# Re-placed weight loads, a 0/1 table for the head gates, and a swapped layout for half of K and V in a gated attention and FFN kernel

## The chip, the cores and the metric

The kernel runs on one core of one Trainium2 chip. The metric is device time in microseconds (us) of that core for one execution. Three runs of the kernel before the change gave 264.25, 263.18 and 264.29, so the median is 264.25. The profile comes from one more execution, which took 264.48; its span (first to last recorded instruction) is 262.7.

## The reference

With x of shape (1, 2048, 512) in bf16, the output is g * a + (1 - g) * b, where g = sigmoid(sum(x * gate_w)) per token.

- b is a gated FFN: `relu(x @ W_gate) * (x @ W_up) @ W_down`, with 1792 hidden columns.
- a is attention with a compressive memory over 4 segments of 512 tokens, 32 heads of width 16:

```python
for s in range(N):
    logits = q_s k_s^T * scale + mask            # causal within the segment
    a_dot = softmax(logits) @ v_s
    a_mem = (phi(q_s) @ M) / (phi(q_s) @ z + 1e-6)
    o_s = g_h * a_mem + (1 - g_h) * a_dot        # g_h = sigmoid(beta), one per head
    M = M + phi(k_s)^T v_s
    z = z + sum(phi(k_s))
a = concat(o_s) @ wo
```

Here phi(t) is t + 1 for t > 0, else exp(t).

## The kernel before the change

**Tiling.** The 2048 tokens are 4 segments (`seg`) of 512. A segment's 512 attention columns are 4 groups (`c`) of 128 columns, that is 8 heads of 16. A *unit* u = 4 * seg + c is one group in one segment, 16 in all. TensorE projects q and k transposed (columns on partitions), and v with tokens on partitions. One unit's heads lie in four 32-row blocks j of the 128 partitions, each with an even head (r = 0) and an odd one (r = 1).

**Scores.** `proj_k` (L567) casts the projected k into `ktr` and writes masked copies into `KT` (L578): the even heads' copy has the odd heads' rows at zero and the other way round, so that a 32-row matmul over a block gives one head's scores. A block of 128 keys has two halves of 64. `KT` holds five half blocks per key block: even half 0, even half 1, even half 0 again (the third masked copy, 256 columns), odd half 0, odd half 1. `qk` (L621) fills 2048 score columns in 4 PSUM banks, one *fill* for a parity r and a half k of the key blocks, four per unit. `qk_diag` (L632) computes for two units the first 64 queries of each key block against `KT[..., 2:4]`, half 0 of the even and of the odd head. `score` (L644) adds a fill or a diagonal to the plan together with the ACT exp that empties the banks (L648); since all of them use the same 4 banks, a score slot on TensorE waits for the exp of the slot before it. There are 72 score slots. GpSimd masks the fills (`mk`, L674): for the queries 64 to 127 of a key block it zeroes the keys that come later.

**PV.** `pv` (L689) multiplies the exps with V: for the fills with `Vp` (128 keys on the partitions, a column of ones behind the 16 of each head), for the diagonals with `Vm`, which `fill_vm` (L609) fills on VectorE from partitions 0 to 63 of `Vp`: even heads to partitions 0 to 63, odd heads to 64 to 127. PV's result is transposed and normalised on VectorE (L722 ff.). `memory` (L810) updates M and z from `pK` (phi(k), transposed by a DMA on SP, L591); `dens` and `recall` (L747, L777) compute the memory's part, with coefficients that go through DRAM on SP's queue (L773, L787).

**Gates.** exp(-beta) is computed on ACT (L401) for all 32 heads; `head_gates` (L385) makes 1/(1+e) and e/(1+e), `row_gates` (L390) picks for each 32-partition block the right heads by 20 small copies in all into `gcat`, and `pair_gates` (L397) spreads them into `bdg`.

**FFN.** `ffn_tasks` (L854): per segment 14 column blocks of gate and up projections (relu on ACT, product on VectorE, `hT`), then 4 token blocks of `out_tile` (L880), which adds hT @ wd and oT @ wo in one bank, scales it on VectorE and stores it.

**Loads.** They are issued ahead of the plan. SP's queue has x (columns 0 to 255 of segment 0, tokens 0 to 255), wq rows 0 to 127, the transposed x columns 256 to 511 (`dma_start_transpose`, L304), wk, wv, pieces of W_gate and W_up, gate_w, beta, the rest of x, the transposed x of segment 1, then `wd_sb` in two loads (L322) and `wo_sb` in seven (L323 to L327). ACT's queue has x (tokens 256 to 511), wq rows 128 to 255, and wq rows 256 to 511 in one load of 256 KB (`load_rows`, L306). The first two 128-column blocks of segment 0's x are turned on TensorE (`x0_tasks`, L498). `proj_q` (L542) for segment 0 runs as a first batch of 8 matmuls on these (wq blocks 0 and 1), and a second batch of 8 that needs the transposed load and wq blocks 2 and 3 (`got_q[2]`, L553).

**Order.** Every piece of work is a task (`plan.add`) with an engine, dependencies and an emit function. The tasks are numbered in the order in which they are added, and `ORDER` (L30) lists these numbers in the order in which they are emitted; each engine, and each DMA queue, runs its own tasks in that order. `UNITS` (L95) says which PSUM bank or ring buffer a task takes. Tasks with `flex` (projections and FFN) are emitted as one 128-column matmul (`full`, L469), or, when the TensorE task before left the array in column mode, as four matmuls of 32 columns side by side (L473). Scores run in row mode, PV, `memory` and `dens` in column mode, `recall` in a mode of its own. The task at L329 only stands for the time that the front loads take; it emits nothing.

Of the kernel before, what the change touches and what calls it, by code (L numbers as in the profile page):

```python
# [7 lines left out]
BF16 = mybir.dt.bfloat16  # L8
# [4 lines left out]
P = 128  # L13
# [165 lines left out]
def kernel(  # L179
# [106 lines left out]
    def load_wd(a, b, name):  # L286
        return load(nc.sync, wd_sb[:, a:b, :],
                    B_W_down.rearrange("(c p) n -> p c n", p=P)[:, a:b, :], name)
# [691 lines left out]
```

## Time and profile before

| | |
|---|---|
| median of three runs | 264.25 us |
| the profiled execution | 264.48 us |
| its span | 262.7 us |
| TensorE matmuls: busy, instructions | 257.8 us (98%), 3828 |
| VectorE: busy, instructions | 204.9 us (78%), 472 |
| ScalarE: busy, instructions | 183.7 us (70%), 168 |
| GpSimd: busy, instructions | 64.2 us (24%), 168 |
| exp of scores, L648 | 64 x 1877 ns and 8 x 1876 ns |
| third masked K, L578 (128x256) | 16 x 298 ns |
| the other two masked K, L578 (128x512) | 16 x 368 ns and 16 x 348 ns |
| small copies of the gates, L393 and L395 | 4 x 161 ns and 16 x 182 ns |
| masks of the fills on GpSimd, L677 | 128 x 452 ns |
| issue of wd and wo on SP | from 21.41 us to 29.64 us |
| TensorE's first matmul on wd | 64.27 us |

How to read it: PE is TensorE, DVE VectorE, ACT ScalarE, POOL GpSimd, SP the engine that issues most DMAs (SPq is its queue). A busy TensorE is not one at its peak, because matmuls overlap and the ends of their rows are modelled: the distance between the starts of two matmuls tells more than the duration of one. A line such as L469 is that of the helper that issues the matmul; which tile it reads tells what it is for. A row in the waits names the waiting engine and line, what it waited for, the total, the number of times and the longest, in us.

### The profile page before, as it was taken

The page shows a single profiled execution, that of the slowest core. Times are in us where ns is not written, and L with a number is a line of the kernel's source. Part 1 is how long each engine was busy: PE and PEld are TensorE (multiplying, and loading weights), DVE is VectorE, ACT ScalarE, POOL GpSimd, SP SyncE. Part 2 cuts the span into 40 slices and gives each one's busy share as a digit, 9 for nine tenths or more (in the row PEclk, how much of TensorE's full clock was granted, in tenths as well). Part 3 has the DMA queues.
Part 4 walks back from the last instruction along what each step waited for, and adds up shares of the span by engine and source line. Part 5 has one row for each costly group of instructions (what it writes and reads, how often), then busy time and mean ns, then how long its engine had stood idle before and what let it go on. Part 6 is the DMA issues. An engine that isn't in the chain of part 4 may idle for free.

```text
span 262.7 us, 8841 instructions
## 1 busy us (share of the span) xinstructions
PE 257.8 (98%) x3828; PEld 117.4 (45%) x3828; DVE 204.9 (78%) x472; ACT 183.7 (70%) x168; POOL 64.2 (24%) x168
## 2 busy tenths in 40 slices
PE   8899999999999999999999999999999999999995
PEld 3344434454444454444444445444444444444454
DVE  2798999999995756959989789676998858688722
ACT  3199889999788678888486776878568759873000
POOL 8022732212321423232031223133121243121000
PEclk9999999999999999999999999999999999999999
DMA  6999984110711201200220111320110200311011
GB/s 146 337 304 323 273 192 53 22 24 10 116 25 52 92 22 39 76 2 2 80 41 4 56 20 36 110 85 2 24 57 3 56 2 22 102 30 73 2 42 42
DMA packets 31566, 19.72 MB, mean 75 GB/s; under 512 B 16040, under 2 KB 29992, under 8 KB 31528
## 3 DMA queue, kind: packets, MB, share of 16 engines
q1 hardware_dynamic: 30840, 18.64, 26.2%
q8 instruction: 30, 0.49, 0.9%
q10 hardware_dynamic: 688, 0.52, 0.9%
q14 instruction: 8, 0.07, 0.1%
HBM read 13.21 MB, written 2.55 MB: 60 GB/s over the span
## 4 chain that ended last, share of the span: by engine, by line
PE 94%; DMA 2%; DVE 2%; SPq 0%; issue 0%
PE ps L469 56%; PE ps L473 20%; PE ps L626 8%; PE ps L699 7%; DMA xT<-in_A_x_dram 2%; PE ps L639 1%; DVE QT L559 1%; PE ps L819 1%; PE ps L795 0%; PE ps L755 0%; SPq L266 0%; DVE KT L578 0%; DVE ktr L575 0%; DVE osr L895 0%
## 5 line engine op out<-in xcount | busy, mean ns | idle before, releaser
L648 ACT ACTIVATE E<-ps 128x2048 bf16<-128x2048 f32 x64 | 120.2, 1877 | 27.3 <-PE ps L626 18.8
L677 POOL TENSOR_SCALAR_AFFINE_SELECT E<-E 128x256 bf16<-128x256 bf16 x128 | 54.8, 452 | 169.8 <-ACT E L648 169.8
L869 DVE TENSOR_TENSOR hT<-ps,rgr 128x512 bf16<-128x512 f32 x56 | 38.0, 684 | 17.0 <-PE ps L469 12.6
L469 PE MATMUL ps<-xT,wu_sb 128*128 128x512 bf16 x168 | 45.9, 380 | 0.0
L469 PE MATMUL ps<-xT,wg_sb 128*128 128x512 bf16 x154 | 42.0, 380 | 0.0
L863 ACT ACTIVATE rgr<-ps 128x512 bf16<-128x512 f32 x56 | 32.5, 599 | 13.4 <-PE ps L473 6.9
L469 PE MATMUL ps<-wd_sb,hT 128*128 128x512 bf16 (+1 forms) x174 | 40.3, 354 | 0.0
L730 DVE STREAM_TRANSPOSE T<-ps 128x512 f32<-128x512 f32 x32 | 22.2, 707 | 7.8 <-PE ps L699 7.7
L626 PE MATMUL ps<-QT,KT 32*128 32x320 bf16 (+3 forms) x512 | 25.4, 273 | 0.1
L469 PEld LDWEIGHTS <-wu_sb 128*128 128x128 bf16 x168 | 15.1, 98 | 18.7 <-issue 2.7
L469 PEld LDWEIGHTS <-hT 128*128 128x128 bf16 x174 | 15.2, 98 | 17.1 <-issue 2.1
L469 PEld LDWEIGHTS <-wg_sb 128*128 128x128 bf16 x154 | 14.4, 98 | 17.7 <-issue 1.3
L895 DVE TENSOR_SCALAR osr<-ps,ngcol 128x512 bf16<-128x512 f32 (+2 forms) x18 | 12.2, 685 | 11.2 <-PE ps L473 5.7
L699 PE MATMUL ps<-E,Vp 128*17 128x320 bf16 (+3 forms) x512 | 19.3, 274 | 0.0
L626 PEld LDWEIGHTS <-KT 32*128 32x128 bf16 x512 | 7.6, 92 | 25.5 <-issue 24.2
L473 PE MATMUL ps<-xT,wg_sb 128*32 128x512 bf16 x280 | 18.6, 379 | 0.0
L648 ACT ACTIVATE Em<-ps 128x2048 bf16<-128x2048 f32 x8 | 15.0, 1876 | 5.0 <-PE ps L639 5.0
L473 PE MATMUL ps<-wd_sb,hT 128*32 128x512 bf16 (+1 forms) x312 | 17.8, 360 | 0.0
L469 PE MATMUL ps<-xT,wq_sb 128*128 128x512 bf16 x60 | 16.4, 382 | 1.0 <-DMA xT<-in_A_x_dram 1.0
L469 PE MATMUL ps<-wv_sb,xT 128*128 128x512 bf16 x62 | 16.9, 380 | 0.0
L559 DVE CAST QT<-ps 128x512 bf16<-128x512 f32 x16 | 10.7, 687 | 6.4 <-PE ps L469 6.2
L473 PE MATMUL ps<-xT,wu_sb 128*32 128x512 bf16 x224 | 15.1, 379 | 0.0
(102 smaller groups left out, 301.3 us busy)
## 6 DMA issues: line engine op xcount, KB each, us to landing
out_dram<-osr SPq DMA_DIRECT2D x15, 128.0 KB
wd_sb<-in_B_W_down_dram SPq DMA_DIRECT2D x2, 896.0 KB
xn<-in_A_x_dram SPq DMA_DIRECT2D x3, 512.0 KB
cdr<-coefs SPq DMA_DIRECT2D x6, 256.0 KB
xn<-coefs SPq DMA_DIRECT2D x6, 256.0 KB
wg_sb<-in_B_W_gate_dram SPq DMA_DIRECT2D x2, 512.0 KB
wu_sb<-in_B_W_up_dram SPq DMA_DIRECT2D x2, 512.0 KB
wg_sb<-in_B_W_gate_dram SPq DMA_DIRECT2D x2, 384.0 KB
```

The source lines that it names most:

```text
L469: nc.tensor.matmul(out, lhsT=lhsT, rhs=rhs, start=start, stop=stop)
L473: nc.tensor.matmul(out[r], lhsT=lhsT[:, r], rhs=rhs, start=start, stop=stop, tile_position=(0, 32 * j))
L559: prj["q", seg, c] = plan.add("DVE", 600, key - RQK, lambda: nc.vector.tensor_copy(QT[i][:], bank(sl)), [a], DVL, frees=[sl])
L626: nc.tensor.matmul(ps[:, j * L + o:j * L + o + L - q], lhsT=KT[i][rows, kb, 3 * r:3 * r + 2].rearrange("p h q -> p (h q)"), rhs=QT[i][rows ...
L639: nc.tensor.matmul(ps[:, o:o + HP], lhsT=KT[i][rows, kb, 2:4].rearrange("p h q -> p (h q)"), rhs=QT[i][rows, kb * P:kb * P + HP], start=Tr ...
L648: last_exp[0] = [plan.add("ACT", 66 + 4 * L / 1.2, key, lambda: nc.scalar.activation(dst, ps[:, 0:4 * L], ACT.Exp, scale=SCALE), [a] + war ...
L677: nc.gpsimd.affine_select(out=m[:, :, o:o + HP], in_=m[:, :, o:o + HP], compare_op=ALU.is_ge, fill=0.0, base=HP, pattern=[[0, 4], [1, HP]] ...
L699: nc.tensor.matmul(bank(sl)[32 * m:32 * m + HW, q:q + w], lhsT=(Vp[i] if n < 4 else Vm)[:, kb, r, 4 * c + j, 0:HW], rhs=rhs, start=(n == 0 ...
L730: done.append(plan.add("DVE", 633, key - RL, lambda r=r, sl=sl: nc.vector.transpose(T[ts.i][:, r], bank(sl)), [a] + done, 75 if r else 0, ...
L863: r = plan.add("ACT", 478, key - RL, lambda sl=gsl, rs=rs: nc.scalar.activation(rgr[rs.i][:], bank(sl), ACT.Relu), [g], ACL, frees=[gsl])
L869: nc.vector.tensor_tensor(hT[hs1.i][:], bank(sl), rgr[rs.i][:], ALU.mult)),
L895: nc.vector.tensor_scalar(osr[os.i][:, n0 - c0:n1 - c0], bank(sl)[:, 0:n1 - n0], ngcol[:, tt:tt + 1], None, ALU.mult)),
```

## The change

Four things are changed, and the order and the bank choice are written anew for them.

1. *Loads.* wq rows 256 to 511 are no longer one load on ACT's queue but two loads of 128 rows on SP's queue, behind the transposed x load. The second batch of the first q projection is split in two by wq block, so that each part waits for its own load. The loads of wd (two) and wo (four tasks) become tasks of the plan, on SP, placed by ORDER.
2. *Gates.* A 0/1 table `pick`, filled by GpSimd with 21 memsets, is multiplied with beta and reduced over the four blocks, so that each partition gets its own heads' beta; exp, 1/(1+e) and e/(1+e) are then computed on the picked values.
3. *K and V.* The even heads' K is stored with its two 64-key halves swapped. The two halves that the diagonal needs are then neighbours (`KT[..., 1:3]`), and the third masked copy goes. The even heads' V for the fills comes from a new tile `Vs` with the same swap, filled by two SBUF-to-SBUF DMAs per segment on SP, each of 64 partitions; the even heads' masks cover partitions 0 to 63 alone.
4. *Planner's figures.* Landing times (`LANDS`) and the placeholder for SP's front time are other numbers.

```diff
-    KT = [sb([P, 4, 5, P // 2], BF16, f"KT{i}") for i in range(RQ)]
+    KT = [sb([P, 4, 4, P // 2], BF16, f"KT{i}") for i in range(RQ)]
+    Vs = sb([P, 4, H // 2, 18], BF16, "Vs")
...
-    got_q = [load(eng, wq_sb[:, ci, :], A_wq[ci * P:(ci + 1) * P, :], "q%d" % ci)
-             for ci, eng in enumerate((nc.sync, nc.scalar))]
+    got_q = [load_wq(nc.sync, 0), load_wq(nc.scalar, 1)]
     nc.sync.dma_start_transpose(out=xT[0][:, NC // 2:NC, :], in_=x[0:L, halves[1]])
     got_x0b = arrival("x0")
-    got_q.append(load_rows(nc.scalar, wq_sb, A_wq, 1, "q"))
+    got_q += [load_wq(nc.sync, ci) for ci in range(2, NC)]
...
-    got_d = [load_wd(0, 7, "d0"), load_wd(7, NF, "d1")]
...
+    def load_late():
+        for j, (f0, f1) in enumerate(((0, 7), (7, NF))):
+            got_d.append(plan.add("SP", 1270, K(2 + j), lambda f0=f0, f1=f1: nc.sync.dma_start(
+                out=wd_sb[:, f0:f1, :],
+                in_=B_W_down.rearrange("(c p) n -> p c n", p=P)[:, f0:f1, :]),
+                lat=5000, xfer=2800.0))
...
+    nc.gpsimd.memset(pick[:], 0.0)
+    for m in range(4):
+        rows = slice(32 * m, 32 * m + 32)
+        nc.gpsimd.memset(pick[rows, 1, :, m], 1.0)
+        for c in range(NC):
+            nc.gpsimd.memset(pick[rows, 0, c, (m + c) % 4], 1.0)
...
+    def pick_heads():
+        nc.vector.tensor_tensor(
+            gsel.rearrange("p k c j r -> p k (c j r)"), pick.rearrange("p k c j r -> p k (c j r)"),
+            betab[:, None, :].to_broadcast([P, 2, H]), ALU.mult)
+        nc.vector.tensor_reduce(out=gcat.rearrange("p k c r -> p (k c) r"),
+                                in_=gsel.rearrange("p k c j r -> p (k c) r j"),
+                                axis=mybir.AxisListType.X, op=ALU.add)
...
     def head_gates():
+        nc.vector.tensor_scalar(rcat[:], gcat[:], 1.0, None, ALU.add)
+        nc.vector.reciprocal(rcat[:], rcat[:])
+        nc.vector.tensor_tensor(gcat[:, 0], gcat[:, 0], rcat[:, 0], ALU.mult)
...
-            a = matmuls(K(-4, c), [got_q[2]] + got_x[0][1], sl, proj_mm(wq_sb, c, 0)[2:], prev=a,
-                        start=False)
+            for ci in range(2, NC):
+                a = matmuls(K(-6 + ci, c), [got_q[ci]] + got_x[0][1], sl,
+                            [proj_mm(wq_sb, c, 0)[ci]], prev=a, start=False, stop=ci == NC - 1)
...
-            for n, (o, w, m, dur) in enumerate([(0, 2, mcol_e, 262), (3, 2, mcol_o, 262),
-                                                (2, 1, mcol_e, 165)])]
+            plan.add("DVE", 262, key + n, lambda n=n, m=m: nc.vector.tensor_scalar(
+                KT[u % RQ][:, :, 2 * n:2 * n + 2],
+                ktr[ks.i].rearrange("p (k h q) -> p k h q", k=4, h=2)[:, :, ::1 if n else -1],
+                m[:, 0:1],
...
+        att["vs", seg] = [plan.add("SP", 600, K(4 * seg - 2 - (1 if seg else 0), 2000), lambda h=h: (
+            nc.sync.dma_start(out=Vs[64 - 64 * h:128 - 64 * h], in_=Vp[i][64 * h:64 * h + 64, :, 0])),
+            [prj["v", seg, t] for t in range(4)] + [att.get(("pv", 4 * seg - 4 + c)) for c in range(NC)],
+            2500, xfer=400.0) for h in range(2)]
...
-        masks += [att["diag", u]] + att["vm", seg]
+        masks += [att["diag", u]] + att["vm", seg] + att["vs", seg]
...
-                            lhsT=(Vp[i] if n < 4 else Vm)[:, kb, r, 4 * c + j, 0:HW],
+                            lhsT=(Vm[:, kb, r] if n > 3 else Vp[i][:, kb, 1] if r else
+                                  Vs[:, kb])[:, 4 * c + j, 0:HW],
```

In the new ORDER, SP's tasks after the front loads begin with: pK of unit 0 (segment 0), the xn load of segment 1, the two V copies of segment 0, pK of unit 2, the second half of wd, three of the wo tasks, pK of unit 1, the transposed x of segment 2, then the first half of wd and the last wo task. The first score slot stands behind six matmuls of the v projection, where it stood right behind those of k.

More of the change, by code (lines that the diff above doesn't have):

```diff
@@ L321, with wo @@
     load_gu(3)
-    got_d = [load_wd(0, 7, "d0"), load_wd(7, NF, "d1")]
-    for c in range(NC):
-        n = P - 32 * c
-        nc.sync.dma_start(out=wo_sb[0:n, c, :], in_=A_wo[(c + 1) * P - n:(c + 1) * P, :])
-        if c:
-            nc.sync.dma_start(out=wo_sb[n:P, c, :], in_=A_wo[c * P:(c + 1) * P - n, :])
-    got_o = arrival("o")
-    plan.add("SP", 28300, -1e9, None, xfer=5900.0)
+    got_d, got_o = [], []
+    plan.add("SP", 22000, -1e9, None, xfer=4500.0)
+    def load_late():
[5 more added lines that the diff above has]
+        for c in range(NC):
+            def wo(c=c, n=P - 32 * c):
+                nc.sync.dma_start(out=wo_sb[0:n, c, :], in_=A_wo[(c + 1) * P - n:(c + 1) * P, :])
+                if c:
+                    nc.sync.dma_start(out=wo_sb[n:P, c, :], in_=A_wo[c * P:(c + 1) * P - n, :])
+            got_o.append(plan.add("SP", 1250 if c else 600, K(4, c), wo, lat=3500, xfer=450.0))
     ident = sb([P, P], BF16, "ident")
@@ L379 @@
     nc.gpsimd.memset(rcol[:], 0.0)
+    nc.gpsimd.memset(pick[:], 0.0)
+    for m in range(4):
+        rows = slice(32 * m, 32 * m + 32)
+        nc.gpsimd.memset(pick[rows, 1, :, m], 1.0)
+        for c in range(NC):
+            nc.gpsimd.memset(pick[rows, 0, c, (m + c) % 4], 1.0)
     def turned(c):
         return [(j, (j - c) % 4) for j in range(4)]
-    def head_gates():
-        nc.vector.tensor_scalar(gall[:, 1], eb[:], 1.0, None, ALU.add)
-        nc.vector.reciprocal(gall[:, 1], gall[:, 1])
-        nc.vector.tensor_tensor(gall[:, 0], eb[:], gall[:, 1], ALU.mult)
@@ L390, in row_gates @@
-    def row_gates(m):
-        g = gall.rearrange("p k (c j r) -> p k c j r", j=4, r=2)
-        rows = slice(32 * m, 32 * m + 32)
-        nc.vector.tensor_copy(gcat[rows, 1], g[rows, 1, :, m])
-        for c in range(NC):
-            nc.vector.tensor_copy(gcat[rows, 0, c], g[rows, 0, c, (m + c) % 4])
-    def pair_gates():
-        for r, m in enumerate((mcol_e, mcol_o)):
-            nc.vector.tensor_scalar(bdg[:, :, r], gcat[:, 1, :, r], m[:, 0:1], None, ALU.mult)
-    got_eb = plan.add("ACT", 200, 0.0, lambda: nc.scalar.activation(
-        eb[:], betab[:], ACT.Exp, scale=-1.0), [got_be], 100)
@@ L403 @@
-    got_gates = plan.add("DVE", 700, 0.0, head_gates, [got_eb], 100, lock=True)
-    got_gates = [plan.add("DVE", 560, 0.0, lambda m=m: row_gates(m), [got_gates], 100, lock=True)
-                 for m in range(4)]
-    got_gates = plan.add("DVE", 300, 0.0, pair_gates, got_gates, 100, lock=True)
+    def pick_heads():
[5 more added lines that the diff above has]
+                                axis=mybir.AxisListType.X, op=ALU.add)
@@ new lines, in head_gates @@
+    def head_gates():
+        nc.vector.tensor_scalar(rcat[:], gcat[:], 1.0, None, ALU.add)
+        nc.vector.reciprocal(rcat[:], rcat[:])
+        nc.vector.tensor_tensor(gcat[:, 0], gcat[:, 0], rcat[:, 0], ALU.mult)
+        for r, m in enumerate((mcol_e, mcol_o)):
+            nc.vector.tensor_scalar(bdg[:, :, r], rcat[:, 1, :, r], m[:, 0:1], None, ALU.mult)
+    got_gates = plan.add("DVE", 380, 0.0, pick_heads, [got_be], 100, lock=True)
+    got_gates = plan.add("ACT", 200, 0.0, lambda: nc.scalar.activation(
+        gcat[:], gcat[:], ACT.Exp, scale=-1.0), [got_gates], 100)
@@ L408 @@
+    got_gates = plan.add("DVE", 850, 0.0, head_gates, [got_gates], 100, lock=True)
     PEL, DVL, ACL, POL = 230, 150, 165, 130
@@ L577, in proj_k @@
         prj["k", seg, c] = [
-            plan.add("DVE", dur, key + n, lambda o=o, w=w, m=m: nc.vector.tensor_scalar(
-                KT[u % RQ][:, :, o:o + w],
-                ktr[ks.i].rearrange("p (k h q) -> p k h q", k=4, h=2)[:, :, 0:w], m[:, 0:1],
+            plan.add("DVE", 262, key + n, lambda n=n, m=m: nc.vector.tensor_scalar(
+                KT[u % RQ][:, :, 2 * n:2 * n + 2],
+                ktr[ks.i].rearrange("p (k h q) -> p k h q", k=4, h=2)[:, :, ::1 if n else -1],
+                m[:, 0:1],
                 None, ALU.mult), [d], DVL,
                 frees=[ks], lock=True)
-            for n, (o, w, m, dur) in enumerate([(0, 2, mcol_e, 262), (3, 2, mcol_o, 262),
-                                                (2, 1, mcol_e, 165)])]
+            for n, m in enumerate((mcol_e, mcol_o))]
         if seg == NSEG - 1:
@@ L626, in qk @@
                 nc.tensor.matmul(ps[:, j * L + o:j * L + o + L - q],
-                                 lhsT=KT[i][rows, kb, 3 * r:3 * r + 2].rearrange(
+                                 lhsT=KT[i][rows, kb, 2 * r:2 * r + 2].rearrange(
                                      "p h q -> p (h q)"),
@@ L638, in qk_diag @@
                     o = j * L + 4 * HP * v + HP * kb
-                    nc.tensor.matmul(ps[:, o:o + HP], lhsT=KT[i][rows, kb, 2:4].rearrange(
+                    nc.tensor.matmul(ps[:, o:o + HP], lhsT=KT[i][rows, kb, 1:3].rearrange(
                                          "p h q -> p (h q)"),
@@ L890, in out_tile @@
                 prev.frees += tuple(h[1] for h in hs[f0:f1])
-            a = matmuls(key, [got_o] + [att["ot", 4 * seg + c] for c in range(NC)], sl, [
+            a = matmuls(key, got_o + [att["ot", 4 * seg + c] for c in range(NC)], sl, [
                 lambda ci=ci, n0=n0, n1=n1: (oT[i][:, ci, lc:lc + P], wo_sb[:, ci, n0:n1])
@@ L917 @@
     got_x[0] = x0_tasks()
+    load_late()
     for seg in range(NSEG):
```

37 lines of the change are left out of this document (19 added, 18 removed), and 124 rows, old and new, of the table ORDER.

## Prediction

> **What bounds the kernel now.** I read the page first, then the waits, then TensorE's timeline against the order of the work, then the DMA stretches at the start. The page's busy shares and its chain name TensorE:
>
> ```profile
> PE 257.8 (98%) x3828; PEld 117.4 (45%) x3828; DVE 204.9 (78%) x472; ACT 183.7 (70%) x168; POOL 64.2 (24%) x168
> ...
> PEclk9999999999999999999999999999999999999999
> ...
> PE 94%; DMA 2%; DVE 2%; SPq 0%; issue 0%
> ```
>
> The clock is full throughout, so the question is only whether TensorE ever waits. In the waits, these are all that are not its own issuing and cost over 0.5 us:
>
> ```profile
> PE ps L469 <- DMA xT<-in_A_x_dram: 1.0, 1, 1.0
> PE ps L914 <- PEq L964: 0.8, 1, 0.8
> PEld L626 <- DVE KT L578: 0.6, 1, 0.6
> PEld L506 <- DMA xn<-in_A_x_dram: 0.6, 1, 0.6
> PEld L469 <- DMA wq_sb<-in_A_wq_dram: 0.6, 1, 0.6
> ```
>
> All belong to the first 13 us. TensorE's timeline there (start, duration, line, count):
>
> ```profile
> 4.75 2.01 PE L469 MATMUL ps<-xT,wq_sb 128*128 128x512 bf16 x8
> 7.73 1.89 PE L469 MATMUL ps<-xT,wq_sb 128*128 128x512 bf16 x8 [0.97 <-DMA xT<-in_A_x_dram]
> 9.45 2.75 PE L469 MATMUL ps<-xT,wk_sb 128*128 128x512 bf16 x12
> 12.34 0.40 PE L626 MATMUL ps<-QT,KT 32*128 32x448 bf16 x8
> ...
> 18.40 0.40 PE L626 MATMUL ps<-QT,KT 32*128 32x320 bf16 x8
> 18.73 2.33 PE L469 MATMUL ps<-xT,wg_sb 128*128 128x512 bf16 x10
> 20.90 0.59 PE L469 MATMUL ps<-xT,wu_sb 128*128 128x512 bf16 x2
> 21.42 0.40 PE L626 MATMUL ps<-QT,KT 32*128 32x320 bf16 x8
> ```
>
> Starts, not durations, show the rate. From 18.73 to 21.42 there are 12 matmuls of 512 columns and one change of tile mode: 2.69 us. The ten that start at 18.73 hand over at 20.90, so one takes 0.217 us; 12 x 0.2165 = 2.60, and the change costs 0.09. A score slot (18.40 to 18.73, with the change behind it) takes 0.33. I added these prices (0.56 for one PV group) along the old ORDER, its numbers turned into tasks by counting the add calls. The start of every score slot then differs from the trace by 1.66 us at the first (12.34) and by 2.25 at the last (234.62), growing by about 0.01 per slot. **So after 12.34 us TensorE never waits for anything.** DVE at 78% and ACT at 70% are beside the path.
>
> **What the change does to TensorE.** The same counting along the new ORDER gives the same matmuls (projections, FFN, scores, PV, memory; only the late half of the first q projection is handed out in single matmuls), the same 72 score slots, the same 173 tasks in column mode, and 151 changes of mode, as before. Shapes stay: a fill reads 128 columns of KT either way, and PV reads 17 columns of Vs in place of Vp. Work on TensorE: **+-0**. What is left to win is the start, and what is left to lose is a new wait.
>
> **The start.** The second batch of q matmuls waits for the transposed load of x (issued at 1.82 on SP). The first batch needs 8 x 0.2165 = 1.73 from 4.75, to 6.48; the second starts at 7.73, so at most **1.25 us** can go. Why the load is late, by stretches (us, engines, clock, DMA share, GB/s):
>
> ```profile
> 4.50:5.00 0.50, 0.50 (x4) 0.28 (x3) 0.43 (x2) 0.45 (x2) 0.49 (x4) 1.00 1.76 259
> 5.00:5.50 0.50, 0.50 (x3) 0.20 (x2) 0.00 (x0) 0.12 (x1) 0.37 (x2) 1.00 1.33 110
> 5.50:6.00 0.50, 0.50 (x4) 0.24 (x3) 0.00 (x0) 0.00 (x0) 0.44 (x5) 1.00 0.25 54
> 6.00:6.50 0.50, 0.50 (x4) 0.15 (x2) 0.00 (x0) 0.00 (x0) 0.50 (x5) 1.00 1.24 204
> ...
> 17.50:18.50 1.00, 1.00 (x9) 0.34 (x11) 0.97 (x6) 1.00 (x3) 0.73 (x2) 1.00 1.27 289
> ```
>
> The transfers nearly stop from 5.0 to 6.0. In the trace's packets, those of the transpose (256 B) and those of wq's rows 256 to 511 on ACT's queue (1 KB) lie side by side from 4.05, and some of both stay open over a microsecond, all to about 6.02. The transposed load of the next segment, alone on its queue, runs at 289 GB/s. The change takes that 256 KB off ACT's queue and puts it behind the transpose on SP's, as two loads. If the company was the cause, x lands after 4.05 + 256 KB at 289 GB/s (0.9) + the 0.6 us that now lie between the last packet (7.1) and the matmul (7.73): 5.6. The two wq blocks follow at 349 GB/s, 0.38 each: 5.9 and 6.3. All are there by 6.48: **-1.25**. Lower bound of the gain: only bytes are moved about, and then the last block lands when x lands now, 7.7; the new order reads it in the second matmul of the batch, so the batch starts at 7.5: -0.2. I take -1.25, because the lone transpose is the nearest row.
>
> The page "DMA: Bandwidth & Descriptors" of the Trainium skill, section "Issuing engines are not separate DMA queues", speaks against it: loads from either engine run on the same DMA engines and interleave, so a change of queue saves only issue time. By it the start would give -0.2 instead of -1.25. The trace agrees as far as both queues' packets interleave here, and not with a mere sharing, since 54 GB/s is far under 349.
>
> **The first score slot.** Now: 7.73 + 20 matmuls x 0.2165 + 0.09 = 12.15, and it starts at 12.34, waiting for KT: **-0.19** if that goes. The new order puts six V matmuls ahead of it. DVE's chain from 6.48: the four QT casts at 0.6 each, the last held by its matmuls to 8.9; two ktr casts from 10.15 to 11.35; two KT at 0.27: 11.9. TensorE comes to 6.48 + 26 x 0.2165 + 0.09 = 12.2. The wait goes, with 0.3 to spare.
>
> **Closer score slots early on.** By the count three slots of unit 0 to 1 come 2.58 us behind the one before; the closest in the trace of before is 2.71. A slot needs its exp finished: 0.46 from slot to exp (12.34 to 12.80) and 1.88 for it, 2.34, plus a handover. Between 0 and 3 x 0.13 = 0.4; I take **+0.1**, nearer to 2.34 + a handover like that from QT's to the next engine's start (0.1 to 0.2).
>
> **Edits at nothing.** The third masked KT (16 x 298 ns, 4.8 us of DVE) goes; its reader's wait ended once in the run on KT, counted above. The gates drop 16 copies of two columns (1.9), four of eight (0.6) and three 32-column operations (0.7); they add a multiply and a reduction over 64 columns (between the 0.16 of L386 and the 0.35 of L738 each) and shorter ones: DVE about 2 us lighter, cover: TensorE waits for none of it. If DVE were the bound, both together would be 7 us. POOL gets 21 memsets of 0.1 (rows of L964 and L354) behind 6.5 us; it then idles 8.2 us to its first mask at 14.74, so they need no cover. Masks over 64 partitions have the same columns: 236 ns (L347, 64 columns) to 452 (L677); POOL waits 169.8 us for exp anyway. wd and wo (2.3 MB) leave the front of SP's queue, where they are issued from 21.4 to 29.6, for plan places before and about unit 1's scores; their first reader is at 64 us. SP's pK transposes, now first at 32.57, move ahead of most of them. The two added wq issues (0.45 each) put wk's issues on SP about 1 us later, 4.2 to 5.2; its 512 KB then land by about 6.3 + 1.5, and its first reader comes at 6.48 + 1.73 = 8.2.
>
> **The V copy** is the one added wait on TensorE's path: PV of a segment's first unit waits for two SBUF-to-SBUF DMAs (147 KB together) on SP. Segment 0: they wait for the last V cast on ACT, behind the fourth exp: score slot at about 20.9, exp to 23.2, cast to 23.7; issues of 0.45 each (rows of L266) to 24.6. Ahead of them in the queue stand a pK transpose and the next xn load (512 KB, 1.5 us), itself behind the four gate sums on DVE; the front loads drain at about 24.5. So they land at about 27.6; the first PV, at 30.84 now, comes at 29.5. Slack 1.9: **0**. Later segments have 12 us and more of TensorE work between the last PV and the next segment's first. Queued behind the copies on SP are pK, wd and wo, due over 20 us later.
>
> **The sum** on the profiled execution (264.48, span 262.7 and 1.8 around it): -1.25 - 0.19 + 0.1 = -1.3, so 263.2. The tail (last matmul 259.39, last cast 259.82) keeps its order. The median shown is 264.25; -1.3 on it is 262.95. Between the two I say **263.1**.
>
> **Rivals.**
> 1. *Only bytes move*: -0.2 - 0.19 + 0.1 = -0.3, about 264.0. For it: 256 KB go to the same engines either way. Against: the near standstill. Chance 0.28.
> 2. *The V copy is late* and TensorE stands at the first PV. Price: each us beyond the 1.9 of slack, one for one. The longest wait shown for a small store to land is 4.0 us (SP's L787 on the store of coefs); 24.6 + 1.5 + 4.0 = 30.1 costs 0.6. It decides from a landing at 29.5 and makes the kernel slower than now from 30.8; a landing at 32.5 gives +1.7, about 265.9. Against: loads in the same stretch land within about 0.6 us of their last packet. Chance 0.15.
> 3. *Forecast*: 263.1, its own range 262.5 to 263.6. Chance 0.57.
>
> A measurement of this kernel tells about 0.5% (1.3 us) from no change, and the forecast lies at that edge: a bit over half of its chance counts as faster, 0.32; the rest with rival 1 is same, 0.54; rival 2 mostly slower, 0.14. Range: 262.4 (no exp cost, all of the start) to 265.2 (part of rival 2).
>
> **What would show it.** The wait of L469 on the load of xT gone or under 0.2; no stretch under 200 GB/s around 5 us; the second q batch near 6.5 and the first score slot near 12.2; the score slots 2.58 apart; the first PV with no DMA named as releaser; 151 changes and PE busy near 257. Wrong: a wait of PV on Vs, of a score slot on exp, or the second batch still at 7.5.

## The result

The kernel after the change takes 264.2 us (median of 22 runs, 263.71 to 265.34); the kernel before, beside it, 263.85 (22 runs). The ratio is 1.0018, 95% interval 1.0010 to 1.0027. In a second comparison (e9 below) the ratio is 1.0001 (0.9987 to 1.0014). So nothing of the forecast gain arrived; the loss lies between nothing and 0.3%. Two of e14's twelve runs, its profiled one (clock 0.66) among them, had a lower granted clock and are left out of its numbers. The profiled execution of after took 264.14, its span is 262.2; before's were 264.48 and 262.7.

The page of after has TensorE as the bound as before, and lighter side engines (VectorE 204.9 to 200.0 us, where the prediction counted 7 less, and GpSimd 64.2 to 62.9):

```profile
PE 255.6 (97%) x3787; PEld 118.0 (45%) x3816; DVE 200.0 (76%) x438; ACT 183.7 (70%) x168; POOL 62.9 (24%) x189
...
PEclk9999999999999999999999999999999999999999
...
PE 94%; DVE 2%; issue 1%; ACT 1%; DVEq 0%; ACTq 0%
```

The chain names no DMA any more. TensorE's timeline at the start (start, duration, line, operands, count):

```profile
0.85 2.82 PE L932 MATMUL ps<-const-bfloat16-1.0 128*128 128x512 bf16 x7 [0.85 <-PEq L983]
...
4.57 4.53 PE L480 MATMUL ps<-xT,wq_sb 128*128 128x512 bf16 x15
8.93 0.59 PE L480 MATMUL ps<-xT,wk_sb 128*128 128x512 bf16 x2
...
11.74 1.24 PE L480 MATMUL ps<-wv_sb,xT 128*128 128x512 bf16 x5
13.13 0.40 PE L642 MATMUL ps<-QT,KT 32*128 32x448 bf16 x8
...
18.75 0.40 PE L642 MATMUL ps<-QT,KT 32*128 32x320 bf16 x8
```

The first row is the *heat*: seven matmuls on constants that run before x has landed, in both kernels. The row of 15 q matmuls has no wait for the load of xT in it, yet it is slow: in the trace its matmuls start 0.40 to 0.43 us apart up to 6.68, and 0.217 apart from 6.99. The ninth, which opens the second batch, starts at 7.42. Before it was 7.73, and the forecast was 6.48. From 7.42, 26 matmuls at 0.2165 and a change of mode make 13.14: the wait for KT is gone. The DMA stretches (clock, DMA share and GB/s are the last three columns) show that the load itself is cured:

```profile
4.50:5.00 0.50, 0.50 (x4) 0.16 (x3) 0.28 (x1) 0.39 (x2) 0.50 (x4) 1.00 1.19 264
5.00:5.50 0.50, 0.50 (x3) 0.22 (x2) 0.00 (x0) 0.00 (x0) 0.36 (x3) 1.00 0.68 205
5.50:6.00 0.50, 0.50 (x3) 0.20 (x2) 0.00 (x0) 0.00 (x0) 0.44 (x5) 1.00 0.82 201
6.00:6.50 0.50, 0.50 (x3) 0.15 (x1) 0.00 (x0) 0.00 (x0) 0.50 (x6) 1.00 1.06 338
```

No stretch is under 200 GB/s, and the transpose's last packet is at 4.97 (7.12 in the profile of before). Note the clock column: it says 1.00 in stretches in which the matmuls run at half rate. The trace also holds records of the granted clock, and the first of them (full clock) only begins at 6.87, at 5.02 in the profile of before; the page and the stretches print full clock where there is no record. The rate has to be read from the starts.

Behind the first score slot nothing is lost or won: from there to the end of the span are 250.35 us before and 249.05 after, and the six V matmuls that now lie ahead of it are 1.30. So the span's 0.5 us are all from the first 13 us. Time and span of the other runs add what one profile can't show. The median span of before is 262.3 to 262.5 in the four comparisons below (29 to 35 runs each), that of after 262.35 here and 262.30 in e9: the profiled 262.7 of before was a late one. And the time outside the span, 1.66 to 1.87 in every one of those runs of before, is over 1.9 in 9 of after's 22 runs, up to 2.75. The spans of the 22 runs of before beside after are not on record, so what part of the ratio 1.0018 lies in the span is not shown.

### The profile page after: what moved, and what is told of

It is laid out like the page before. It is cut to its first block, busy times and chain, and to the rows that moved or that the text cites. A ratio compares the mean times of both kernels' runs of the same rounds, so it can differ in the third digit from the quotient of the medians.

```text
span 262.2 us, 8798 instructions
## 1 busy us (share of the span) xinstructions
PE 255.6 (97%) x3787; PEld 118.0 (45%) x3816; DVE 200.0 (76%) x438; ACT 183.7 (70%) x168; POOL 62.9 (24%) x189
## 4 chain that ended last, share of the span: by engine, by line
PE 94%; DVE 2%; issue 1%; ACT 1%; DVEq 0%; ACTq 0%
PE ps L480 56%; PE ps L484 20%; PE ps L642 8%; PE ps L716 7%; PE ps L932 1%; PE ps L655 1%; ACT E L664 1%; PE ps L837 1%; DVE T L748 1%; DVE ktr L587 0%; PE ps L773 0%; DVE osr L913 0%; PE ps L813 0%; PE ps L517 0%; DVE pkT L545 0%
## 5 line engine op out<-in xcount | busy, mean ns | idle before, releaser
L694 POOL TENSOR_SCALAR_AFFINE_SELECT E<-E 128x256 bf16<-128x256 bf16 (+1 forms) x128 | 52.8, 435 | 169.7 <-ACT E L664 169.6
L480 PE MATMUL ps<-xT,wg_sb 128*128 128x512 bf16 x162 | 44.9, 380 | 0.4 <-issue 0.2
L480 PE MATMUL ps<-xT,wu_sb 128*128 128x512 bf16 x150 | 41.8, 380 | 0.6 <-issue 0.5
L480 PE MATMUL ps<-wd_sb,hT 128*128 128x512 bf16 (+1 forms) x157 | 37.1, 351 | 0.6 <-issue 0.5
L480 PEld LDWEIGHTS <-wg_sb 128*128 128x128 bf16 x170 | 15.8, 98 | 19.7 <-issue 1.9
L480 PEld LDWEIGHTS <-hT 128*128 128x128 bf16 x164 | 14.0, 98 | 16.2 <-issue 3.4
L484 PE MATMUL ps<-wd_sb,hT 128*32 128x512 bf16 (+1 forms) x352 | 20.7, 362 | 0.0
L484 PE MATMUL ps<-xT,wu_sb 128*32 128x512 bf16 x264 | 17.6, 379 | 0.0
L480 PE MATMUL ps<-xT,wq_sb 128*128 128x512 bf16 x56 | 16.5, 403 | 0.3 <-issue 0.2
L480 PE MATMUL ps<-xT,wk_sb 128*128 128x512 bf16 x57 | 15.8, 380 | 0.4 <-issue 0.2
L484 PE MATMUL ps<-xT,wg_sb 128*32 128x512 bf16 x216 | 14.5, 379 | 0.0
```

The costliest lines, as they stand in the source:

```text
L480: nc.tensor.matmul(out, lhsT=lhsT, rhs=rhs, start=start, stop=stop)
L484: nc.tensor.matmul(out[r], lhsT=lhsT[:, r], rhs=rhs, start=start, stop=stop, tile_position=(0, 32 * j))
L694: nc.gpsimd.affine_select(out=m[half, :, o:o + HP], in_=m[half, :, o:o + HP], compare_op=ALU.is_ge, fill=0.0, base=HP if r else 0, pattern ...
```

## The experiments

"Outside" is a run's time less its span. All comparisons are with runs of before on the same chip; before's median there was 263.85 for after, 264.02 for e1 to e4, 264.17 for e5 to e8, 264.22 for e9 to e12 and 264.19 for e13 to e15.

| run | time, median | ratio to before (95%) | span, median | outside over 1.9 | TensorE instructions |
|---|---|---|---|---|---|
| after | 264.2 | 1.0018 (1.0010 to 1.0027) | 262.35 | 9 of 22 | 7648 |
| e1 before again | 263.87 | 0.9991 (0.9977 to 1.0006) | 262.15 | 0 of 12 | 7669 |
| e2 before, wq on SP | 264.05 | 1.0000 (0.9988 to 1.0013) | 262.30 | 0 of 12 | 7669 |
| e3 after, wq on ACT | 264.0 | 0.9999 (0.9986 to 1.0011) | 262.05 | 6 of 12 | 7648 |
| e4 after, wd and wo in front | 275.77 | 1.0434 (1.0409 to 1.0459) | 274.0 | 1 of 4 | 7648 |
| e5 after, more code | 264.19 | 0.9999 (0.9987 to 1.0011) | 262.40 | 0 of 11 | 7668 |
| e6 before, less code | 263.57 | 0.9976 (0.9965 to 0.9986) | 261.85 | 0 of 12 | 7649 |
| e7 = e3 and e5 | 264.01 | 0.9990 (0.9981 to 0.9999) | 262.30 | 0 of 12 | 7668 |
| e8 after, little heat | 264.99 | 1.0033 (1.0017 to 1.0048) | 263.15 | 4 of 12 | 7636 |
| e9 after again | 264.2 | 1.0001 (0.9987 to 1.0014) | 262.30 | 3 of 12 | 7648 |
| e10 = e5, V ahead of x | 263.74 | 0.9983 (0.9973 to 0.9994) | 262.00 | 0 of 11 | 7668 |
| e11 = e5, no wait for V | 264.19 | 1.0007 (0.9990 to 1.0025) | 262.45 | 0 of 12 | 7665 |
| e12 before, still less code | 263.44 | 0.9983 (0.9967 to 0.9998) | 261.40 | 7 of 12 | 7641 |
| e13 = e11 | 264.65 | 1.0023 (1.0008 to 1.0039) | 262.85 | 0 of 12 | 7665 |
| e14 = e13, V ahead of x | 265.14 | 1.0035 (1.0017 to 1.0053) | 263.40 | 0 of 10 | 7665 |
| e15 = e10, W_gate piece earlier | 263.74 | 0.9990 (0.9981 to 0.9999) | 262.00 | 0 of 12 | 7668 |

e6 and e12 leave work out, so only their last two columns are of use. e11, e13 and e14 leave out the swapped V: the even heads read `Vp`, whose keys are in another order than the scores'.

**The loads alone.** e1 is before unchanged. e2 gives before the new place of the wq loads, e3 gives after the old one:

```diff
# e2, on before
-    got_q.append(load_rows(nc.scalar, wq_sb, A_wq, 1, "q"))
+    for ci in range(2, NC):
+        nc.sync.dma_start(out=wq_sb[:, ci, :], in_=A_wq[ci * P:(ci + 1) * P, :])
+    got_q.append(arrival("qb"))
# e3, on after
-    got_q += [load_wq(nc.sync, ci) for ci in range(2, NC)]
+    nc.scalar.dma_start(out=wq_sb[:, 2:4, :],
+                        in_=A_wq.rearrange("(c p) n -> p c n", p=P)[:, 2:4, :])
+    got_q += [arrival("q%d" % ci) for ci in range(2, NC)]
```

> The kernel before, unchanged, for a second trace and the spread of its spans. Theory A (the start decides: when x lands and when TensorE's clock becomes full, both varying from run to run): spans spread over about 1 us, their median near 262.0, below the 262.7 of the profile shown; the second q batch starts below 7.73, near 7.0. Theory B (the start is as in the profile shown, and the changed kernel loses outside its span): spans near 262.7 and the second batch near 7.7 again.

> The kernel before with one part of the change: wq rows 256 to 511 as two loads on SP's queue behind the transposed x. If the arrival of x bounds the start: 1.0 to 1.25 us faster than before. Theory A: x lands by 5.6 as in the changed kernel, but the first batch of q matmuls runs at half rate until the clock is full, so the second batch starts between 6.5 and 7.5 and the time is 0 to 0.5 faster than before. Theory B: no difference, within 0.1.

> The changed kernel with wq rows 256 to 511 loaded on ACT's queue in one piece, as before. If the re-placing is worth what was forecast: 1.0 us or more slower than the changed kernel, about 265.2. Theory A: the wait for x comes back beside a cold first batch, 0 to 0.5 slower, 264.2 to 264.7. If the two more issues on SP are what costs: 0.3 faster, 263.9.

Measured: the move decides the landing in either kernel. The transpose's last packet is at 5.42 in e2 and, back on the old place, at 6.85 in e3. It does not move the time in either. One reason is in e1, whose profile is another execution of the same kernel (the two rows from 4.82 are e2's):

```profile
4.56 4.14 PE L469 MATMUL ps<-xT,wq_sb 128*128 128x512 bf16 x16
8.54 2.75 PE L469 MATMUL ps<-xT,wk_sb 128*128 128x512 bf16 x12
11.43 0.40 PE L626 MATMUL ps<-QT,KT 32*128 32x448 bf16 x8
...
4.82 3.72 PE L471 MATMUL ps<-xT,wq_sb 128*128 128x512 bf16 x16
...
11.26 0.40 PE L628 MATMUL ps<-QT,KT 32*128 32x448 bf16 x8
```

In e1 x's last packet came at 6.19, the second batch started at 6.81 and the first slot at 11.43, all 0.9 us ahead of the profile that the prediction was made from, with no change at all. Every later slot is 0.91 or 0.92 earlier too, and the span is as much shorter (261.8). e2's profile has the start that the prediction wanted: no wait for x, the second batch at 6.64 and the first slot at 11.26. That is 1.08 ahead of the profile of before, but only 0.17 ahead of e1, and from the first slot to the end it takes 250.79, 0.44 more than before. The 0.44 go between 39.3 and 41.4 us, where TensorE waits for VectorE, and VectorE has waited 0.6 for a load of x: there, too, a later load takes part of an early start back.

**The late loads.** e4 puts the loads of wd and wo back in front of the plan:

> The changed kernel with the loads of wd and wo issued in front of the plan, as before; the V copies then queue behind them on SP. Theory A (start): no difference from the changed kernel, 264.2 +- 0.15, unless the first PV now waits for the V copy: those land after 33, the PV is due at 30.4, so up to 3 us slower, about 267. If the late loads are what costs: 0.3 faster, 263.9.

Measured: 275.77, four times the loss expected. SP issues the V copies at 34.63 in place of 24.65, behind the loads, and PV stands:

```profile
29.36 0.40 PE L643 MATMUL ps<-QT,KT 32*128 32x448 bf16 x8
39.40 1.03 PE L717 MATMUL ps<-E,Vs 128*17 128x448 bf16 x16 [9.64 <-DMA Vs<-Vp]
```

The next matmuls are slow too (1.03 us for a row that takes 0.61 in after): the record of the granted clock says 0.50 from 34.27 to 44.51, so the long wait is paid a second time at half rate behind it. So with V copies on SP, wd and wo have to leave SP's front.

**The end of the code.** In the trace, one DMA queue fetches TensorE's instructions in packets of 16 KB, 30 in a run for some 7660 instructions, so about 256 a packet (a matmul is two: the weight load and itself). In the profile of after, the stretch from 262.2 us, where the span ends, to 265 holds one packet, of that queue, at 263.53:

```profile
DMA packets 1, 0.02 MB, mean 6 GB/s; under 512 B 0, under 2 KB 0, under 8 KB 0
...
q8 instruction: 1, 0.02, 2.1%
```

In the profile of before the last one comes 4.49 us ahead of the end, in e1 4.59. The change has 21 fewer TensorE instructions: 24 weight loads and matmuls fewer, because the new ORDER emits four more projection or FFN products as one matmul in place of four, and three waits more. e5 gives 20 of them back without more columns, e6 takes 20 from before:

```diff
# e5, on after: heat
-            w = L if k < 6 else P
-            nc.tensor.matmul(bank(warm[k])[:, 0:w], ...
+            for a, w in ([(0, 172), (172, 172), (344, 168)] if k < 5 else
+                         [(0, L)] if k < 6 else [(0, P)]):
+                nc.tensor.matmul(bank(warm[k])[:, a:a + w], ...
# e6, on before: out_tile passes this to matmuls, which skips those of the list
+                    left_out=(1, 3) if tt == 0 and f0 < 10 else ())
# e12
+                    left_out=(1, 3) if tt == 0 or tt == 1 and f0 == 10 else ())
```

> The kernel after, with five of the seven heat matmuls cut into three pieces of the same total width: 10 more TensorE matmuls, 20 more TensorE instructions (7668 where after has 7648 and before 7669), the same columns. Theory A (the end of the code): TensorE's code comes in 16 KB blocks, and in the profile of after the last block is fetched 1.35 us behind the last recorded instruction, in the profiles of before about 4.5 us ahead of it; the execution then waits for that fetch in some runs. A expects the time outside the span back at 1.7 to 1.8 in all runs (none over 1.9, where after had 9 of 22), the last fetch some 3 to 5 us ahead of the end, the span as after's (262.0 to 262.6), the time 264.0. Rival B (the added copies, memsets or late loads cause the time outside the span): 4 to 6 of 12 runs stay over 1.9.

> The kernel before, with 10 matmuls of the first token block's product with wd left out (tokens 0 to 127 of the output lack 4 of the 14 column blocks of the FFN): TensorE has 7649 instructions, one more than after. Theory A (the end of the code): 4 to 6 of 12 runs have over 1.9 us outside the span, the mean goes from 1.72 to about 1.95, though nothing else of the change is in this kernel. Rival B (the added copies, memsets or late loads): none over 1.9. The span falls by the work left out, some 1 us or less.

> The kernel before with more matmuls with wd left out (four of 14 blocks for tokens 0 to 127 and part of them for tokens 128 to 255): 7641 TensorE instructions. Those with runs over 1.9 us outside the span have 7648 and 7636, those without have 7649 (the same matmuls left out in the first token block alone), 7668 and 7669. If the place of a block's boundary against the end of the code is the cause and it lies between 7648 and 7649, 3 to 6 of 12 runs are over 1.9 here. If it is something else of the change that only the extra instructions cover up, none is.

Measured: e5 loses the long runs altogether (outside 1.68 to 1.80) at an unchanged span, and its last packet is back at 4.53 ahead of the end. e6, at 7649, did not do what theory A expected: no run over 1.9, packet at 4.06 ahead. e12, at 7641, has them (7 of 12, mean 2.00), with nothing of the change in it, and its packet comes 1.06 us behind the end. Over all kernels, those with 7649 instructions or more have no run over 1.9, those with 7648 or fewer have 30 of 74. So the number of TensorE instructions alone turns the long runs on and off.

The profiles tie the time to the packet. In after, e9 and e12 it ends 2.26, 2.41 and 2.36 us behind the span, and the time outside the span is 1.96, 2.10 and 2.06: each time 0.31 less. In e8 it ends only 1.33 behind, and the time outside is 1.71, as without it. So an execution waits for this packet when it is late enough. Why the last fetch comes late with fewer instructions, and not in every run, is not shown: at 7648, e4's profile has it 3.6 ahead of the end, and e3's shows only 29 packets. It costs after 0.2 us on average in the first comparison (1.94 against 1.73), 0.07 in e9 (1.80), and up to 1 in one run.

The page "Runtime: NRT & Kernel Launch" of the Trainium skill, section "Instruction fetch mechanics", has the 16 KiB blocks of 256 instructions and says that the cost of a boundary is mostly hidden. The trace agrees on the blocks, and names no wait for the 29 packets inside the span; the one at the end is not hidden.

**The clock.** e8 leaves one heat matmul of 128 columns of the seven:

> The kernel after, with one heat matmul of 128 columns in place of seven (3200 columns). Theory C (the clock ate the start's gain: until 5.0 to 6.9 us the matmuls run at half rate, 0.427 us in place of 0.217): without heat they run at half rate to 8 us or later, each of those us costs half, so the span is 1 to 3 us longer than after's (263.3 to 265.3), and the second q batch starts near 8. Rival D (the loads' arrival sets the start, the clock does not matter): the span stays within 0.3 of after's 262.35. TensorE has 7636 instructions, 12 fewer than after; theory A of the runs above then has the last block fetched behind the end or not at all, and says nothing sure of the time outside the span.

```profile
4.69 5.27 PE L480 MATMUL ps<-xT,wq_sb 128*128 128x512 bf16 x15
...
14.00 0.40 PE L642 MATMUL ps<-QT,KT 32*128 32x448 bf16 x8
```

Measured: the 15 q matmuls take 5.27 us for 4.53, the clock record begins at 8.49, the second batch is at 8.08 though x had landed at 5.35, and the median span is 0.8 longer. That is just under the range expected and well over the rival's 0.3: the clock binds the start of after. e9, after once more, is the other end; its record begins at 4.00:

> The kernel after, unchanged, beside the three below on the same chip. Theory A (the end of the code): 4 to 6 of 12 runs over 1.9 us outside the span. Theory V (rival 2 of the prediction, in small): the V copies of segment 0 land at the edge of the first PV; their packets ended at 29.43 where PV started at 30.38, and at 30.20 where it waited 0.7 to 0.9 and started at 31.17. In this profile PV starts within 0.9 to 1.05 of the copies' last packet, or earlier than that only if they end before 29.3. Time 264.2 to 264.4, span 262.35 median.

```profile
4.66 3.71 PE L480 MATMUL ps<-xT,wq_sb 128*128 128x512 bf16 x15
...
12.67 0.40 PE L642 MATMUL ps<-QT,KT 32*128 32x448 bf16 x8
...
16.02 0.60 PE L480 MATMUL ps<-wv_sb,xT 128*128 128x512 bf16 x2
16.90 0.60 PE L480 MATMUL ps<-xT,wg_sb 128*128 128x512 bf16 x2 [0.28 <-DMA wg_sb<-in_B_W_gate_dram]
...
18.74 0.40 PE L642 MATMUL ps<-QT,KT 32*128 32x320 bf16 x8
```

With the same program and the same heat the 15 matmuls take 3.71; the ninth starts at 6.56, as forecast (6.48). Across the profiles of kernels with full heat the record begins anywhere from 3.55 to 6.87, or the matmuls are at full rate from the first. The page "TensorE: Matmul & The Clock Gate" of the Trainium skill, section "Part 1: The HAM clock gate (the "warmup" mystery)", says that the array runs at half rate until a free-running window of some 3.4 us has been busy, so that the same kernel warms at a different moment in each run; the 0.427 and 0.217 us and a scatter from run to run agree with it, though the scatter here, 3.55 to 6.87, is wider than the 500 ns to either side that the section also gives. One thing stays open: the heat has the same columns in all these kernels, yet the record begins later than 5.36 in six of the ten profiles of kernels made from after and in none of the five made from before. Whether that is chance is not shown.

**What an early start is worth.** The lines of e9 above also show where its 0.46 us at the first slot go: at 16.45 TensorE is ready for the second piece of W_gate, which is not there before 16.90, and the third slot (18.74) is where it was in after (18.75). e10 shows the same: first slot at 12.66, the piece's first matmul at 16.98, third slot at 18.82. Part of an early start is gone before that. In e11 the second batch starts at 6.47, just as forecast, but weight loads of TensorE then wait 0.80 us for wk and 0.61 for wv, and the first slot is at 13.09, where after has it with a second batch 0.95 later; W_gate's piece comes at 17.34, the third slot at 19.17, and the early start has become a loss. In e9 a weight load waits 0.49 for wq and one 0.58 for wk, and the first slot is at 12.67, where 12.2 was forecast. SP issues this piece at 8.5 to 9.2 in these kernels, behind wq's 256 KB and two more issues. In e7, which has wq on ACT's queue, it is issued at 7.72, and an early start stays early:

```profile
12.35 0.40 PE L644 MATMUL ps<-QT,KT 32*128 32x448 bf16 x8
...
16.15 0.59 PE L482 MATMUL ps<-xT,wg_sb 128*128 128x512 bf16 x2
...
17.97 0.40 PE L644 MATMUL ps<-QT,KT 32*128 32x320 bf16 x8
```

> The kernel after, with wq rows 256 to 511 in one load on ACT's queue as before the change, and the 20 more TensorE instructions of the run above. With after's plan that load gave a span of 262.05 (median) and a mean of 2.02 outside it. Theory A: 1.75 outside the span in all runs, the time 263.8, 0.2 to 0.3 below before. Rival B: 264.0, with half of the runs over 1.9 outside.

e7's time, 264.01, is rival B's figure and not theory A's 263.8, though none of its runs is over 1.9 outside, as A expected. Its profile has a span of 261.4, but the median is 262.30: with wq on ACT's queue x lands at 6.05 here and at 6.85 in e3, so other runs may pay there, which no trace of them shows. e5 and e7 are the plainest test of the forecast -1.25: on the same chip they differ in wq's loads alone, and the new place (e5) takes 264.19 where the old one takes 264.01. e15 moves the piece itself:

```diff
+    f0, f1 = FP[1]
+    nc.sync.dma_start(out=wg_sb[:, :, f0:f1],
+                      in_=B_W_gate.rearrange("(c p) n -> p c n", p=P)[:, :, f0:f1])
     nc.sync.dma_start(out=gwb[:], in_=gate_w.partition_broadcast(P))
...
-    load_gu(1)
+    got_g[1] = arrival("g1")
+    got_u[1] = load_cols(nc.sync, wu_sb, B_W_up, *FP[1], "u1")
```

> The kernel of e10 (after, 20 more TensorE instructions, x load behind the V copies) with the second piece of W_gate (512 KB) issued ahead of gate_w (128 KB to all partitions) and beta. Theory G (an early start is given back at this piece, which lands at 16.9 to 17.3 whenever the start is early): the piece lands 0.4 us earlier or more, its wait goes, the third score slot comes at 18.3 to 18.5 where the first is at 12.6, and the span's median is 0.2 to 0.4 below e10's, 261.6 to 261.8; the time 263.4. Rival: 262.0, another load is late in its place.

Measured: 262.00, e10's figure, as the rival had it. Its profile can't say why: the wait for W_gate is gone and a weight load waits 0.3 for W_up, but the start was late anyway (first slot 13.09), and from the first to the third slot it takes 5.62, as in after, so nothing is lost there. That one piece earlier makes another one late is not shown.

**The V copies.** In after's profile their packets end at 29.43 and PV starts at 30.38 without a wait; in e5's they end at 30.20, and PV waits:

```profile
30.08 0.40 PE L642 MATMUL ps<-QT,KT 32*128 32x448 bf16 x8
31.17 0.61 PE L716 MATMUL ps<-E,Vs 128*17 128x448 bf16 x16 [0.69 <-DMA Vs<-Vp]
```

In both PV starts 0.95 to 0.97 after the last packet, so after's copies come just in time. From the fifth to the ninth score slot, where this PV lies, e5 takes 12.27 us, e9 11.64 and after 11.54; the kernels whose copies land early (e3, e7, e10, e15) take 11.50. So the copies cost 0.77, 0.14 and 0.04 in these executions. In e3 and e7 the packets end at 28.02 and 27.45. e10 moves the load of segment 1's x behind the copies, e11 and e13 take the wait away, e14 does both:

```diff
# e10, on e5: ORDER
-    227 240 127 224 132 66 228 345 117 120 121 92 37 40 41 38 79 674 46 229 130 243 230 244 133
+    227 240 127 224 132 66 228 117 120 121 345 92 37 40 41 38 79 674 46 229 130 243 230 244 133
# e11, on e5
-        masks += [att["diag", u]] + att["vm", seg] + att["vs", seg]
+        masks += [att["diag", u]] + att["vm", seg]
-                            lhsT=(Vm[:, kb, r] if n > 3 else Vp[i][:, kb, 1] if r else
-                                  Vs[:, kb])[:, 4 * c + j, 0:HW],
+                            lhsT=(Vm if n > 3 else Vp[i])[:, kb, r, 4 * c + j, 0:HW],
```

> The kernel after with 20 more TensorE instructions in the heat (as above, to keep the end of the code off the block's boundary), and in ORDER the load of segment 1's x (512 KB) moved from ahead of the two V copies of segment 0 to behind them. Theory V: the copies land 1.2 to 1.7 us earlier, about 27.5 to 28.5, no PV waits for them, and the median span falls by the wait that runs of after have on average, 0.2 to 0.5, to 261.9 to 262.2; the time 263.6 to 263.9. Rival (the wait seen once is a rare run): the span stays at 262.4, the time 264.1.

> The kernel after with the 20 more TensorE instructions, ORDER as in after, the V copies still issued, but PV of the even heads reads V in place and does not wait for them (so the even heads' output is that of keys in the wrong order). This is the price of the wait alone. Theory V: median span 261.9 to 262.2 (after and the same with more code: 262.35 and 262.40), the time 263.6 to 263.9. Rival: 262.4 and 264.1.

> The kernel of e11 once more (PV of the even heads reads V in place and does not wait for the copies; 20 more TensorE instructions; the x load of segment 1 ahead of the copies). Theory V (the wait sets the median): 261.9 to 262.1 span. Theory L (the loads of the start set it, from run to run, and the wait rarely counts): 262.3 to 262.5 again, the profile with waits on loads of wk, wv or wg before 18 us.

> Both: the x load of segment 1 behind the V copies in ORDER as in e10, and no wait for the copies as in e11 (even heads read V in place). Theory V: as e10, 262.0, and as e13. Theory X (the place of the x load counts in another way than by V): 262.0 here, 262.4 in e13. Theory L (the loads of the start): 262.3 to 262.5 here too, e10's 262.0 would then have been chance.

Measured: e10's spans lie at 261.8 to 262.4 and e15's, with the same place of x, at 261.7 to 262.4, against 262.0 to 263.0 of e5 and 261.7 to 263.7 of e9; 0.3 at the median against e9, on the same chip as e10, as theory V said. But e11 and e13 gave 262.45 and 262.85, and their spans scatter from 261.8 to 264.1, where e10's and e15's keep within 0.7; e14 scatters as they do (262.0 to 264.4; its profile is not used). So without the wait, in this form, nothing was saved, and theory V is not confirmed by its own subtraction. Why these three scatter is open: the profiles of e11 and e13, at 262.5 and 262.2, show waits of 0.2 to 0.8 on loads before 18 us, and behind it no wait that explains spans of up to 264.1. What is shown is that PV does wait in some executions (e5), and that the kernels with x behind the copies are 0.17% (e10) and 0.10% (e15) faster than before, where after and e5 are not. That the wait for V is what they save is not shown.

## Why the prediction was wrong, point by point

- **TensorE's work +-0**: right. The distance from the first slot to the end is the same to 0.01 us, the six V matmuls counted.
- **The start, -1.25**: this term failed. The load did what was forecast (last packets at 4.96 to 5.55 in all kernels with wq on SP, with the 0.6 us from there to the matmul that makes an estimate of 5.6 to 6.1, where 5.6 was forecast). The second batch came at 7.42 and not 6.48: the profile gained 0.31 of the 1.25. Over the kept profiles it starts at 7.19 on average with wq on ACT's queue (six profiles, 6.65 to 7.73) and at 6.91 with it on SP's (nine with full heat, 6.47 to 7.42), so the term is worth some 0.3 at the second batch, and at the median span nothing. Three things were missing from the step. First, "The clock is full throughout": it rested on the clock row, which shows full where the clock has no record; the first batch was taken at 0.2165 a matmul, and it runs at 0.427 up to a moment that differs from run to run. Before, the wait for x covers part of this: in e1's profile the first batch ends at 6.7, and the wait ends at 6.81. (In the profile of before, too, the first matmul took 0.34, so at most 1.13 could go, not 1.25.) Second, the price was read from one execution in which x was late; e1's profile has the second batch at 6.81, so 0.92 of the 1.25 was not in every run of before to be won. Third, the load stream behind: wk was to land by 7.8 for a reader at 8.2, but where the second batch starts as early as forecast, wk's matmuls wait (to 8.46 in e9, 8.59 in e11), then those on wv (e11), and I did not follow the queue on to W_gate's second piece at 16.5 to 17. There an early start is given back (e9, e10) or more than given back (e11).
- **KT's wait, -0.19**: right. **Closer slots, +0.1**: three slots come 2.59 us behind the one before, where the count gave 2.58, and the distance from the first slot to the end shows no cost. The +0.1 should have been 0.
- **Edits at nothing** (third KT, gates, memsets, masks): right, none is on the path. VectorE became 4.9 us lighter and not the 7 counted; 0.9 of the difference are the two masked K left, which take 12.0 in place of 11.1.
- **The V copy, 0**: the profile of after has no wait, but the 1.9 us of slack were not there. The packets ended 1.8 us behind the forecast 27.6, since the front loads end at 26.30 and not 24.5. (The two copies move 144 KB each, 288 KB together, and not 147 together.) Rival 2 happens in small: PV waits 0.69 us in e5's profile.
- **"1.8 around it"**: taken as fixed. It is not: with the shorter code the last fetch can end behind the span, 0.07 to 0.2 us on average (after, e9; gone in e5, there without the change in e12). With spans about equal at the median that makes the time up to 0.1% longer; the rest of the first comparison's 1.0018 is open.
- **Rival 1** (only bytes move, -0.2 at the start) came nearest to the time, by luck: it said that the last bytes would land as late as now, but x landed 2 us earlier and the gain went elsewhere. The Trainium skill's rule that queues of different engines share the same DMA engines (the page "DMA: Bandwidth & Descriptors", section "Issuing engines are not separate DMA queues") would have given the better time here; the landing itself did depend on where wq's rows stood, 4.96 to 5.55 with them behind the transpose on SP's queue against 6.05 to 7.12 beside it on ACT's.

## What to carry to other kernels

A wait in one profile is not a gain until a second execution shows it, and until the next late thing is priced: behind a cured load stand the clock of TensorE and every later load of the same queue, each with its own first reader. Read TensorE's rate from the starts of its matmuls, not from the clock row, above all in the first 10 us. Keep each run's time beside its span: a difference between the two is outside all engine rows, and here it came from the number of instructions.

## What was not expected of the hardware

- A fetch of TensorE code behind the end of the span, up to 1 us of time in after (1.2 in e12), switched on by taking 21 to 33 of 7669 TensorE instructions away (20 were not enough, e6) and off by 20 more with the same columns. Where it is late, the time outside the span is its end less 0.31.
- Kernels with the same heat start their q matmuls at half rate for a time that ends between 3.55 and 6.87 us, or run at full rate from the first q matmul; the same program, after, at 6.87 in one execution and 4.00 in another.
- The transposed load's last packet comes at 6.05 to 7.12 beside 256 KB on ACT's queue, at 4.96 to 5.55 ahead of them on SP's.
- In e4 TensorE stands for 9.64 us until 39.40, and its granted clock is 0.50 from 34.27, inside that wait, until 44.51, 5.1 us after it works again.
